# A list scheduler that counts DMA by packets and lanes, other places for the loads of z and v, and one pair of token blocks that stays in SBUF

## The chip, the cores and the metric

The kernel runs on one core of a Trainium2 chip. The metric is the device time of one execution in microseconds (us), the median of several runs. On the core work five engines with a queue of their own each: TensorE (PE in the profile) multiplies, VectorE (DVE) and ScalarE (ACT) do the elementwise work, GpSimd (POOL) and SyncE (SP) here mostly issue transfers.

## The reference

Three stages stand one behind the other. x is what one stage hands to the next: 6016 rows (tokens) of 256.

```
scores = (1/S) * z @ z.T                 # per batch, S = 3008, z is S x 64
x      = u * (maximum(scores, 0)**2 @ v) # attention, u and v are S x 256
g      = s * maximum(x @ w_in, 0)**2 + b # first MLP, 256 -> 2048
x      = g @ w_out                       # 2048 -> 256
h      = x @ w2_in                       # second MLP
out    = (h * sigmoid(1.702 * h)) @ w2_out
```

All of it is float32. No operand goes into TensorE as it is: each is split into a high part (a cast to a shorter format) and a low part (the rest), and a product is made of three matmuls: high by high, high by low, low by high. ACT makes the high parts (a cast, "hi"), DVE the low ones (a subtraction, "lo").

## The kernel before, in words

**Tiles.** The 3008 tokens of a batch are cut into five blocks of 512 and one of 448. The twelve blocks of both batches are numbered m = 0 to 11; 0 to 4 and the short 10 belong to the first batch, 5 to 9 and the short 11 to the second, and they are finished in the order 0, 1, 2, 3, 4, 10, 5, 6, 7, 8, 9, 11. For the MLPs two neighbours make a pair: pair p holds the blocks 2p and 2p+1, so pair 4 is blocks 8 and 9, and pair 5 the two short ones.

**Attention.** z is loaded transposed in pieces of 32 (tile zr, line 341), turned by DVE (zt, line 359), and split into zq and zk (lines 368 and 371 for zk). A tile holds the same 64 rows of z twice, in its upper and its lower 64 partitions. For the two first tiles of the first batch both halves are loaded; for the others the lower half is copied from the upper one by a transfer inside SBUF (line 351). Tiles of v are loaded (vr, line 411) and split (lines 427 and 431). Scores go into ps_s (line 511), are clipped and squared on ACT (lines 515 and 518), split (lines 522 and 526) and multiplied by v into accA or accB (lines 450, 451, 455). A score tile that another block needs transposed is turned by DVE (T, line 551), stored to DRAM (H<-T, line 566, POOL) and fetched again later (R<-H, line 579, SP) and split once more (lines 601 and 605). `gate` multiplies a block's sum by u (gx, line 911), `store_rows` writes it to DRAM, `fetch_rows` reads it again as f when its pair enters the first MLP.

**Weights.** While attention runs, the weights of both MLPs are prepared: `wr` is loaded (lines 632 to 638), taken apart and rounded on DVE and ACT (lines 645 to 732, "decode"), and stored in the forms that a seven-product scheme for 2 x 2 blocks needs (uf, dw, df, POOL). These operations are called free: nothing waits for them before the MLPs begin.

**MLPs.** For each layer and each pair, `up` (896 KB each, line 775) and `d` tiles are loaded, products go into ps_a to ps_d (line 1045), are combined, activated, split (lines 1164 and 1168) and multiplied down into the accumulators (line 1238). The last pair of the second layer ends the program: its parts are closed (line 1308), turned (line 984) and stored (line 997).

**What sets the order.** The program writes a list of operations with a cost each. `ordered` is a list scheduler: it runs through the list with a clock for each engine, its own prices for operations and transfers, due times that follow from what PE needs, and a count of free buffers (56 cells of 128 x 512, 13 "big", 5 "wide" ones, banks of the accumulators). It returns one fixed order for each engine. At run time only semaphores hold an instruction back, and an engine does not step past one that waits. SP issues loads, POOL issues stores. Each queue that issues DMAs goes round eight lanes: a DMA may wait for the one issued eight before it.

## Time and profile before

| | us |
|---|---|
| median of three runs (lowest, highest) | 1436.26 (1430.92, 1436.39) |
| the profiled execution | 1433.64 |
| its span, first to last instruction | 1431.9 |
| PE busy in the span | 1395.0 |
| DVE busy | 1312.7 |
| ACT busy | 1190.9 |

The profiled execution lies between the runs; 1.7 us of its time are outside the span. Busy PE is not PE at its peak, since a matmul at half clock counts as busy for longer. The rows of the trace use the line numbers of the kernel before.

### The profile page before, as it was taken

The page shows a single profiled execution, that of the slowest core. Times are in us where ns is not written, and L with a number is a line of the kernel's source. Part 1 is how long each engine was busy: PE and PEld are TensorE (multiplying, and loading weights), DVE is VectorE, ACT ScalarE, POOL GpSimd, SP SyncE. Part 2 cuts the span into 40 slices and gives each one's busy share as a digit, 9 for nine tenths or more (in the row PEclk, how much of TensorE's full clock was granted, in tenths as well). Part 3 has the DMA queues.
Part 4 walks back from the last instruction along what each step waited for, and adds up shares of the span by engine and source line. Part 5 has one row for each costly group of instructions (what it writes and reads, how often), then busy time and mean ns, then how long its engine had stood idle before and what let it go on. Part 6 is the DMA issues. An engine that isn't in the chain of part 4 may idle for free.

```text
span 1431.9 us, 20300 instructions
## 1 busy us (share of the span) xinstructions
PE 1395.0 (97%) x6147; PEld 1150.3 (80%) x6147; DVE 1312.7 (92%) x2324; ACT 1190.9 (83%) x2308; POOL 165.1 (12%) x260
## 2 busy tenths in 40 slices
PE   7999999999999799999999999999999999999997
PEld 4788889778887688887888778988887887878896
DVE  5998978999997699999999999898988999989996
ACT  6998866999876498998999898988888796968784
POOL 0022111131221100101001000000020202020201
PEclk9999999999999899999999999999999999999999
DMA  8698998688989976776757576666758474646644
GB/s 188 187 307 261 243 252 231 214 271 259 290 256 274 269 262 228 261 232 231 258 185 266 181 255 219 217 229 212 243 159 289 153 264 159 234 155 224 192 149 110
DMA packets 175949, 324.71 MB, mean 227 GB/s; under 512 B 61376, under 2 KB 96256, under 8 KB 172000
## 3 DMA queue, kind: packets, MB, share of 16 engines
q1 hardware_dynamic: 153104, 245.30, 56.6%
q0 software_dynamic: 19072, 77.45, 14.7%
q10 hardware_dynamic: 3664, 0.68, 0.3%
q8 instruction: 48, 0.79, 0.2%
q14 instruction: 61, 0.50, 0.1%
HBM read 243.93 MB, written 78.12 MB: 225 GB/s over the span
## 4 chain that ended last, share of the span: by engine, by line
PE 72%; DMA 8%; DVE 7%; issue 7%; ACT 4%; SPq 1%; POOL 1%; ACTq 0%; DVEq 0%; POOLq 0%
PE ps_d L1045 8%; PE ps_b L1045 7%; PE ps_c L1045 7%; PE accB L1238 6%; PE ps_b L1238 5%; PE ps_a L1045 4%; DMA R<-H 4%; PE accB L450 3%; PE accB L451 3%; PE ps_s L511 3%; PE accB L455 3%; PE accA L1238 3%; PE ps_c L1238 3%; PE accA L451 3%; PE accA L450 3%
## 5 line engine op out<-in xcount | busy, mean ns | idle before, releaser
L1168 DVE TENSOR_TENSOR lo<-g_c,hi 128x512 fp32r<-128x512 f32 (+1 forms) x540 | 346.1, 672 | 15.9 <-ACT hi L1164 15.2
L1164 ACT CAST hi<-g_c 128x512 fp32r<-128x512 f32 (+1 forms) x540 | 310.5, 618 | 3.7 <-DVE g_c L1153 1.2
L515 ACT ACTIVATE a<-ps_s 128x512 f32<-128x512 f32 (+1 forms) x168 | 100.2, 607 | 39.4 <-PE ps_s L511 39.3
L1045 PE MATMUL ps_b<-op_t,up 128*128 128x512 f32 (+1 forms) x432 | 121.3, 389 | 2.2 <-DVE g_c L1119 1.0
L1045 PE MATMUL ps_d<-op_t,up 128*128 128x512 f32 (+1 forms) x432 | 120.7, 387 | 0.4 <-DVE g_c L1119 0.4
L451 PE MATMUL accA<-hi,v 128*128 128x512 f32 x288 | 114.1, 396 | 6.2 <-DVE v L431 6.1
L450 PE MATMUL accB<-hi,v 128*128 128x512 f32 (+1 forms) x288 | 111.2, 386 | 5.2 <-ACT hi L522 5.2
L526 DVE TENSOR_TENSOR lo<-a,hi 128x512 fp32r<-128x512 f32 (+1 forms) x156 | 104.2, 672 | 11.5 <-ACT hi L522 11.0
L450 PE MATMUL accA<-hi,v 128*128 128x512 f32 x288 | 112.8, 392 | 0.5 <-ACT hi L522 0.2
L1131 ACT ACTIVATE g_c<-g_c 128x512 f32<-128x512 f32 (+1 forms) x144 | 89.5, 623 | 28.3 <-DVE g_c L1119 28.0
L451 PE MATMUL accB<-hi,v 128*128 128x512 f32 (+1 forms) x288 | 110.8, 385 | 0.0
L518 ACT ACTIVATE a<-a 128x512 f32<-128x512 f32 (+1 forms) x168 | 107.7, 650 | 1.1
L511 PE MATMUL ps_s<-zq,zk 128*128 128x512 f32 (+1 forms) x336 | 103.6, 395 | 4.5 <-DVE zk L371 3.9
L522 ACT CAST hi<-a 128x512 fp32r<-128x512 f32 (+1 forms) x168 | 105.7, 636 | 0.9
L1153 DVE TENSOR_TENSOR g_c<-g_c,g_c 128x512 f32<-128x512 f32 (+1 forms) x156 | 104.9, 672 | 1.5
L997 POOL DMA_DIRECT2D out_dram<-o x84 | 53.9, 649 | 404.1 <-DVE o L979 383.3
L1045 PEld LDWEIGHTS ps_b<-op_t,up 128*128 128x128 f32 x432 | 79.9, 188 | 21.5 <-DVE g_c L1119 3.4
L1238 PE MATMUL accB<-hi,d 128*128 128x512 f32 (+1 forms) x312 | 95.0, 386 | 0.0
L1045 PEld LDWEIGHTS ps_d<-op_t,up 128*128 128x128 f32 x432 | 80.4, 188 | 17.8 <-DVE g_c L1119 1.9
L1134 ACT ACTIVATE g_c<-g_c 128x512 f32<-128x512 f32 (+1 forms) x144 | 88.4, 629 | 0.7
L551 DVE STREAM_TRANSPOSE T<-a 128x512 f32<-128x512 f32 x120 | 83.9, 702 | 5.2 <-ACT a L518 4.8
L455 PE MATMUL accB<-lo,v 128*128 128x512 f32 (+1 forms) x276 | 83.8, 385 | 3.2 <-DVE lo L526 3.2
(172 smaller groups left out, 3460.0 us busy)
## 6 DMA issues: line engine op xcount, KB each, us to landing
up<-uf SPq DMA_DIRECT2D x96, 896.0 KB
H<-T POOLq DMA_DIRECT2D x30, 1024.0 KB, 7.2
R<-H SPq DMA_DIRECT2D x120, 256.0 KB
d<-dw SPq DMA_DIRECT2D x114, 256.0 KB
d_s<-df1s SPq DMA_DIRECT2D x54, 256.0 KB
f<-rows SPq DMA_DIRECT2D x20, 512.0 KB
d_s<-df0s SPq DMA_DIRECT2D x72, 128.0 KB
d_s<-df0s SPq DMA_DIRECT2D x36, 256.0 KB
```

What stands on the lines that cost most here:

```text
L450: nc.tensor.matmul(T[k][:, :n], w[:, 0, cols], T[hi][:, :n], **start_flags(k, fresh))
L451: nc.tensor.matmul(T[k][:, :n], w[:, 1, cols], T[hi][:, :n], **start_flags(k, ()))
L455: nc.tensor.matmul(T[k][:, :n], w[:, 0, cols], T[lo][:, :n], **start_flags(k, ()))
L511: nc.tensor.matmul(T[self.p][:, :n], k, T[zq][:, h, :n], start=h == 0, stop=h == 1)
L518: nc.scalar.activation(out=T[self.a][:, :n], in_=T[self.a][:, :n], func=AF.Square)
L522: nc.scalar.copy(out=T[self.hi][:, :n], in_=T[self.a][:, :n])
L526: nc.vector.tensor_tensor(out=T[self.lo][:, :n], in0=T[self.a][:, :n], in1=T[self.hi][:, :n], op=ALU.subtract)
L1045: nc.tensor.matmul(to[:, :n], a[h], y[:, g, :n], start=first and j == 0, stop=False, skip_group_check=True)
L1153: nc.vector.tensor_tensor(out=self.get(to), in0=self.get(x), in1=self.get(y), op=ALU.subtract)
L1164: nc.scalar.copy(out=T[keys[0]][:, :n], in_=self.get(c))
L1168: nc.vector.tensor_tensor(out=T[keys[1]][:, :n], in0=self.get(c), in1=T[keys[0]][:, :n], op=ALU.subtract)
L1238: nc.tensor.matmul(to[:, :n], w[:, h, cols], g[:, :n], start=first and j == 0, stop=False, skip_group_check=True)
```

## The change

The work on PE, DVE and ACT is the same, operation for operation (6147 matmuls before and now). What changes is the order, and some transfers.

1. **`ordered` and `moves`.** A transfer is now priced by its packets and its count of DMAs, with eight lanes per queue in the scheduler's model. A load is not placed earlier than `HOLD` = 4 us before the modelled transfer queue gets to it, unless it is due. The free decode operations get two windows each of the scheduler's clock in place of one: 45 to 235 and 300 to 370 us for the first layer's weights, 200 to 235 and 300 to 800 us for the second's (before: 20 to 450 and 200 to 800), and do not start ahead of the first.
2. **`load_z`.** In the first batch both halves of every tile are loaded from DRAM. In the second batch the copy inside SBUF is issued by POOL, not by SP.
3. **`load_v`.** The first batch's tiles of v but the first are issued by POOL.
4. **`KEPT` and `PAIRS`.** Blocks 8 and 9 are not stored and fetched again: the first MLP's operands are made from gate's own tile. Both MLPs take the pairs in the order 4, 0, 1, 2, 3, 5.
5. **`tail_of`.** For the pair that ends the program the products come in another order: one whole product (c11) behind P5 and P6 in place of ahead of P5, and c22 by halves at the end, beside c12.

```
+HOLD = 4
...
+            if op.pipe:
+                t = max(t, min(pipe - HOLD, latest[i] - 2.0), lanes[op.engine == "POOL"][0])
...
-        clocks[e] = s0 + op.cost
+        end, late = s0 + op.cost, op.late
+        if op.pipe:
+            time, land, lane = s0, 0.0, lanes[e == "POOL"]
+            for _ in range(op.count):
+                time = max(time, lane.pop(0))
+                pipe = max(pipe, time + 0.4) + op.pipe / op.count
+                time += op.cost / op.count
+                lane.append(max(time + 1.9, pipe + 1.7))
+                land = max(land, lane[-1])
+            end = time
+            late = land - end
...
-        twice = bb == 0 and t < 2
+        twice = bb == 0
...
-            move(128, lambda: nc.sync.dma_start(out=T[key][64:], in_=T[key][:64]), [key], [key])
+            move(128, lambda: nc.gpsimd.dma_start(out=T[key][64:], in_=T[key][:64]), [key], [key], engine="POOL")
...
+        queue = "POOL" if bb == 0 and c else "SP"
...
+    KEPT = (8, 9)
...
-        store_rows(0, m, key)
+        if m not in KEPT:
+            store_rows(0, m, key)
...
-        fs = [("f", layer, 2 * p + y) for y in range(2)]
+        fs = [("x" if layer == 0 and 2 * p + y in KEPT else "f", layer, 2 * p + y) for y in range(2)]
...
-        line = parts("c22", "P1") + late + whole("c11") + parts("t1", "P5")
+        line = parts("c22", "P1") + late
         if pair.ending:
-            line += parts("t2", "P6") + whole("c22") + parts("t3", "P7") + whole("c21")
+            line += parts("t1", "P5") + parts("t2", "P6") + whole("c11") + parts("t3", "P7") + whole("c21")
             line += close(0, 0, "v") + close(0, 1, "w")
             for d, x in enumerate(("s1", "u3")):
-                line += whole("c12", (d,)) + close(1, d, x)
+                line += whole("c22", (d,)) + whole("c12", (d,)) + close(1, d, x)
...
+    PAIRS = (4, 0, 1, 2, 3, 5)
...
-        [(20.0, 450.0), (200.0, 800.0)],
+        [[(45.0, 235.0), (300.0, 370.0)], [(200.0, 235.0), (300.0, 800.0)]],
```

Three places show what the new order is. A row is an instruction: its line, its kind, the tile it writes and what it reads. The first place is SP's queue at the very start; zr is z, vr is v, wr are the weights of the first MLP, and the number behind the name is the tile of the batch. Before:

```order
L341 DMA zr_2_185<-in_z_dram 32x16x32 x2
L411 DMA vr_1_188<-in_v_dram 32x4x256 x4
L341 DMA zr_3_193<-in_z_dram 32x16x32 x2
L411 DMA vr_2_199<-in_v_dram 32x4x256 x4
L636 DMA wr_0_214<-in_moe_w_in_dram 128x1x256 x2
L638 DMA wr_0_214<-in_moe_w_out_dram 128x512
L341 DMA zr_4_236<-in_z_dram 32x16x32 x2
L411 DMA vr_3_246<-in_v_dram 32x4x256 x4
L636 DMA wr_1_261<-in_moe_w_in_dram 128x1x256 x2
L638 DMA wr_1_261<-in_moe_w_out_dram 128x512
L351 DMA zr_2_185<-zr_2_185 64x512
```

and now:

```order
L356 DMA zr_0_168<-in_z_dram 32x16x32 x2
L356 DMA zr_1_178<-in_z_dram 32x16x32 x4
L429 DMA vr_0_183<-in_v_dram 32x4x256 x2
L356 DMA zr_2_203<-in_z_dram 32x16x32 x4
L356 DMA zr_3_232<-in_z_dram 32x16x32 x4
L356 DMA zr_4_289<-in_z_dram 32x16x32 x4
```

The copy of z tile 2 (L351) stood behind three loads of v and two of weights; now no copy is left in the first batch, the v tiles have gone to POOL, and the weights come behind all of z.

The second place is ACT's queue in the first microseconds, where v_0 and v_1 are the parts of the first and second tile of v. Before:

```order
L368 CAST zk_0_206<-zt_0_197 128x512
L427 CAST v_0_0_210<-vr_0_175 128x256
L427 CAST v_0_1_212<-vr_0_175 128x256
L427 CAST v_0_2_219<-vr_0_175 128x256
L427 CAST v_0_3_225<-vr_0_175 128x256
L515 ACTIVATE a<-ps_s 128x512 x2
```

and now:

```order
L445 CAST v_1_0_201<-vr_1_171 128x256
L445 CAST v_1_1_208<-vr_1_171 128x256
L383 CAST zk_0_212<-zt_0_193 128x512
L445 CAST v_1_2_215<-vr_1_171 128x256
L445 CAST v_1_3_218<-vr_1_171 128x256
L383 CAST zk_1_230<-zt_1_221 128x512
L533 ACTIVATE a<-ps_s 128x512 x2
```

Two casts of the second tile of v, which POOL loads now, stand ahead of the cast of zk_0 that the first scores need. On DVE one subtraction of the same tile (v_1_0) stands likewise ahead of the two that the first scores need.

The third place is SP's queue where attention ends; R_5 are the last stored score tiles that block 11 fetches, f_0 and f_1 the stored rows of the pair that was first, ur is u. Before:

```order
L579 DMA R_5_1_4905<-H_5_1_3920 32x4x512 x4
L579 DMA R_5_2_5029<-H_5_2_4295 32x4x512 x4
L856 DMA f_0_5097<-rows_0_123 128x1024
L856 DMA f_1_5120<-rows_1_124 128x1024
L579 DMA R_5_3_5188<-H_5_3_4675 32x4x512 x4
L775 DMA up_0_0_5214<-uf_75 128x1792
L632 DMA wr_7_5226<-in_moe_w_in_dram 128x2x256
L638 DMA wr_7_5226<-in_moe_w_out_dram 128x512
L579 DMA R_5_4_5236<-H_5_4_5034 32x4x512 x4
```

and now:

```order
L650 DMA wr_7_5130<-in_moe_w_in_dram 128x2x256
L656 DMA wr_7_5130<-in_moe_w_out_dram 128x512
L597 DMA R_5_2_5150<-H_5_2_4287 32x4x512 x4
L597 DMA R_5_3_5205<-H_5_3_4695 32x4x512 x4
L597 DMA R_5_4_5253<-H_5_4_5010 32x4x512 x4
L793 DMA up_4_0_5304<-uf_75 128x1792
L793 DMA up_4_1_5332<-uf_76 128x1792
```

The two f loads are gone, the last weight tile has moved ahead of R_5_2, and the first `up` load behind R_5_4.

## Rows read from the trace of the kernel before

**Rows 1.** Page of the kernel: busy time of each engine.

```profile
PE 1395.0 (97%) x6147; PEld 1150.3 (80%) x6147; DVE 1312.7 (92%) x2324; ACT 1190.9 (83%) x2308; POOL 165.1 (12%) x260
```

**Rows 2.** Windows: stretch, length, busy us of five engines, granted clock, DMA share, GB/s.

```profile
36.00:99.40 63.40, 62.32 (x268) 49.23 (x268) 63.03 (x121) 61.99 (x124) 9.92 (x16) 1.00 0.80 243
99.40:240.00 140.60, 140.60 (x633) 118.45 (x632) 120.64 (x226) 107.24 (x206) 19.39 (x30) 1.00 0.91 247
274.00:292.00 18.00, 16.80 (x66) 11.57 (x65) 17.88 (x40) 17.61 (x39) 4.97 (x8) 1.00 0.66 226
446.00:482.00 36.00, 27.12 (x111) 22.10 (x111) 25.02 (x46) 20.12 (x41) 2.70 (x4) 0.86 1.02 259
482.00:1421.80 939.80, 934.14 (x4159) 776.46 (x4158) 879.39 (x1496) 800.23 (x1538) 84.41 (x130) 1.00 0.64 217
```

**Rows 3.** Timeline of the first 13 us: start, duration, engine, instruction, [idle before it].

```profile
0.75 0.91 SPq L341 DMA_DIRECT2D zr<-in_z_dram  x2
...
4.53 0.71 DVE L359 STREAM_TRANSPOSE zt<-zr 128x512 f32<-128x512 f32 x1 [3.34 <-DMA zr<-in_z_dram]
...
6.72 1.33 ACT L427 CAST v<-vr 128x256 fp32r<-128x256 f32 x4 [0.83 <-DMA vr<-in_v_dram]
...
7.27 2.20 PE L511 MATMUL ps_s<-zq,zk 128*128 128x512 f32 x8
...
12.05 1.20 PE L511 MATMUL ps_s<-zq,zk 128*128 128x512 f32 x4 [2.57 <-DVE zk L371]
```

**Rows 4.** Timeline from 20 to 34 us, the copy of z and what waits.

```profile
27.89 0.71 DVE L359 STREAM_TRANSPOSE zt<-zr 128x512 f32<-128x512 f32 x1 [5.00 <-DMA zr<-zr]
...
28.64 0.62 ACT L368 CAST zk<-zt 128x512 fp32r<-128x512 f32 x1 [4.94 <-DVE zt L359]
...
28.96 0.79 PE L451 MATMUL accA<-hi,v 128*128 128x512 f32 x1 [5.06 <-DVE v L431]
...
33.96 0.62 ACT L368 CAST zk<-zt 128x512 fp32r<-128x512 f32 x1 [3.18 <-DVE zt L359]
```

**Rows 5.** Timeline of the end of attention, 455 to 482 us.

```profile
455.78 4.70 SPq L579 DMA_DIRECT2D R<-H  x4
461.46 1.67 ACT L601 CAST hi<-R 128x512 fp32r<-128x512 f32 x3 [3.55 <-DMA R<-H]
470.15 0.43 DVE L645 TENSOR_SCALAR pw<-wr 128x512 uint32<-128x512 uint32 x1 [3.08 <-DMA wr<-in_moe_w_out_dram]
471.50 1.11 PE L455 MATMUL accB<-lo,v 128*128 128x448 f32 x2 [3.20 <-DVE lo L526]
474.76 0.62 ACT L601 CAST hi<-R 128x512 fp32r<-128x512 f32 x1 [7.14 <-DMA R<-H]
476.79 0.74 PE L450 MATMUL accB<-hi,v 128*128 128x448 f32 x1 [4.18 <-ACT hi L522]
```

**Rows 6.** Timeline of DVE, two neighbours in a stretch without idle time.

```profile
442.26 0.68 DVE L526 TENSOR_TENSOR lo<-a,hi 128x512 fp32r<-128x512 f32 x1
442.86 0.41 DVE L682 TENSOR_TENSOR zeros<-zeros,wf 128x256 f32<-128x256 f32 x1
```

**Rows 7.** POOL's group of stores (busy us, mean ns), and DMA issue to landing.

```profile
L997 POOL DMA_DIRECT2D out_dram<-o x84 | 53.9, 649 | 404.1 <-DVE o L979 383.3 <-DVE o L984 16.4 <-DVE g_c L1153 3.7
...
out_dram<-o POOLq DMA_DIRECT2D x80, 64.0 KB, 4.8
```

**Rows 8.** Timeline of the last 12 us.

```profile
1419.51 0.99 PE L1213 MATMUL accA<-hi,d 128*128 128x448 f32 x4
...
1420.27 0.62 DVE L1296 TENSOR_TENSOR k_w<-ps_d,k_p 128x448 f32<-128x448 f32 x1 [4.38 <-ACT k_u L1280]
...
1421.78 0.37 PE L1213 MATMUL accB<-lo,d 128*128 128x448 f32 x1
...
1424.55 0.60 DVE L984 STREAM_TRANSPOSE o<-k_u 128x448 f32<-128x448 f32 x1
```

**Rows 9.** Waits of SP's queue from 482 to 1421.8 us: total, times, longest.

```profile
SPq L775 <- PE ps_d L1045: 267.2, 44, 15.3
```

More of the change, by code (lines that the diff above doesn't have):

```diff
@@ L92, in ordered @@
     extra = [i for i in range(n) if ops[i].free]
-    for which, (a, b) in enumerate(spread):
+    for which, windows in enumerate(spread):
         some = [i for i in extra if ops[i].free == which + 1]
+        whole = sum(b - a for a, b in windows)
         for x, i in enumerate(some):
-            latest[i] = a + (b - a) * x / len(some)
+            t = whole * x / len(some)
+            for a, b in windows:
+                if t < b - a:
+                    break
+                t -= b - a
+            latest[i] = a + t
     for i, op in enumerate(ops):
@@ L110, in ordered @@
     waiting = [len(b) for b in before]
-    ready, calm = [0.0] * n, [0.0] * n
+    ready, calm = [0.0] * n, [spread[op.free - 1][0][0] if op.free else 0.0 for op in ops]
     pending = {e: [] for e in clocks}
@@ L185, in ordered @@
                 u[1] -= 1
-                u[2] = max(u[2], s0 + op.cost + late)
+                u[2] = max(u[2], end + late)
                 if u[1] == 0:
@@ L192, in ordered @@
             waiting[j] -= 1
-            t = s0 + (lag(i, j) if not op.pipe else op.cost + late)
+            t = end + late if op.pipe else s0 + lag(i, j)
             ready[j] = max(ready[j], t)
@@ L280, in attention_mlp_mlp_kernel, with put @@
     ops, T = [], {}
-    def put(engine, cost, late, f, reads=(), writes=(), new=(), adds=(), free=0, due=None, pipe=0, soon=None):
-        ops.append(Op(engine, cost, late, f, reads, writes, new, adds, free, due, pipe, soon))
+    def put(engine, cost, late, f, reads=(), writes=(), new=(), adds=(), free=0, due=None, pipe=0, soon=None, count=1):
+        ops.append(Op(engine, cost, late + pipe, f, reads, writes, new, adds, free, due, pipe, soon, count))
     def scalar(n, f, reads=(), writes=(), new=(), **more):
@@ L289, in vector, with moves @@
         put("DVE", 0.065 + (0.00056 if fast else 0.00105) * n, 0.14, f, reads, writes, new, **more)
-    def carry(kb, run):
-        return kb * 1024 / run * (0.0185 + run / 27200) / 16
     STORES = "POOL"
     to_hbm = dict(SP=nc.sync, POOL=nc.gpsimd)[STORES]
-    def move(kb, f, reads=(), writes=(), new=(), engine="SP", run=2048, **more):
-        put(engine, 0.75 if engine == "POOL" else 0.45, 2.0, f, reads, writes, new, pipe=carry(kb, run), **more)
-    def moves(kb, fs, reads=(), writes=(), new=(), engine="SP", run=2048, count=None, **more):
+    def moves(kb, fs, reads=(), writes=(), new=(), engine="SP", run=2048, count=None, slow=1.0, **more):
         def f():
@@ L303, in f, with move @@
                 g()
-        put(engine, (0.75 if engine == "POOL" else 0.45) * (count or len(fs)), 2.0, f, reads, writes, new, pipe=carry(kb, run), **more)
+        count = count or len(fs)
+        pipe = 1.05 * slow * kb * 1024 / run * (0.0085 + run / 27200) / 16
+        put(engine, (0.7 if engine == "POOL" else 0.45) * count, 2.0, f, reads, writes, new, pipe=pipe, count=count, **more)
+    def move(kb, f, *args, **more):
+        moves(kb, [f], *args, **more)
     def matmuls(count, n, f, reads=(), adds=(), writes=(), new=()):
@@ L1513, in write_list @@
         for layer in range(2):
-            for p in range(NP):
+            for p in PAIRS:
                 parity[layer, p] = flip
```

43 lines of the change are left out of this document (22 added, 21 removed).

## The prediction, made before the change was run

> **What bounds the kernel now.** I read the page first. PE is busy for 1395.0 of 1431.9 us [rows 1], so some 37 us of the span are without a matmul, and the matmuls that ran at half clock come on top. No work leaves PE, so the question is which of these microseconds the new order gives back. Windows show that they are not spread evenly. From 99 to 240 us PE is never idle [rows 2]. In the 940 us of the MLPs it misses 5.7 (939.80 less 934.14), 0.6%. What is left lies in four places: the first 60 us, a small one near 280, the end of attention, and the last 10 us.
>
> *The start.* A timeline shows DVE waiting 5.00 us, until 27.89, for the copy of a z tile inside SBUF, and ACT 4.94 us for the turned tile; PE then starts again after 5.06 us [rows 4]. Another copy costs ACT 3.18 us more, until 33.96 [rows 4]. From 36 to 99 us DVE has 0.4 us of idle time and ACT 1.4, PE 1.1 [rows 2]: these two set the pace until they have caught up. So what the copies cost is what the two engines that pace the stretch lost, 4.94 + 3.18 = 8.1 us, and not the larger gap on PE.
>
> *Near 280.* Between 274 and 292 us DVE works 17.88 of 18.00 us, ACT 17.61, and PE misses 1.2 [rows 2].
>
> *The end of attention.* Of 36 us from 446 on PE misses 8.9, at a mean granted clock of 0.86 [rows 2]. The 0.86 are 36 x 0.14 = 5.0 us of lost clock; the level is half (1.2 GHz) for twice that, some 10 us, from about the matmul at 471.50 that followed 3.20 us of waiting. As 4.2 to 4.8 of these 10 us were idle in any case, the slow matmuls themselves cost some 2.6. Loss here: 8.9 + 2.6 = 11.5. The chain is read backwards: PE waits 4.18 us for a cast on ACT; ACT stood before it for 7.14 us until 474.76 at a cast of R, for the transfer issued from 455.78 on; and PE's 3.20 us came from DVE, which stood for 3.08 us at a weight tile [rows 5]. An engine in program order that waits for a late load holds up the small split behind it, for which PE waits.
>
> *The last 10 us.* The last matmul starts at 1421.78, the last turn of DVE ends at 1425.15 [rows 8], and transfers run to 1431.9.
>
> **The change part by part.**
>
> *z and v, first 60 us.* Every z tile of the first batch comes from DRAM in whole, and no load waits for another: the 8.1 us of waits go. Against it, the first scores now stand behind the second tile of v, from POOL. POOL issues four DMAs at 0.65 us each [rows 7] from about 0.8 us, so until 3.4. For the landing I have no row of this load. The quick end is the first z tile: issued until 1.7, turned at 4.53 [rows 3], 2.9 us. The slow end is POOL's small stores in full traffic, 4.8 us [rows 7]. So it lands at 6.3 to 8.2. Then one cast of 256 columns on ACT (four take 1.33, so 0.33 [rows 3]), and on DVE one subtraction of 256 and two of 512, at most 0.41 and, by the starts in [rows 6], 0.60 each: together 1.9 us, first scores at 8.2 to 10.1 in place of 7.27 [rows 3]. Part of the 0.9 to 2.8 comes back: the four casts of v no longer stand between the cast of zk_0 and that of zk_1, and the 2.57 us at 12.05 [rows 3] shrink as the second tile of z is loaded at once. I take 1.2 us net (bounds 0 and 2.2). The matmuls that idle to keep PE warm end at about 7.6, so PE waits 0.6 to 2.5 us; after the 2.57 us at 12.05 the next ones ran at full clock (four in 1.20) [rows 3], after 5.06 at half (one in 0.79) [rows 4], so I expect full clock. Sum of the start: 8.1 - 1.2 = 6.9 us gained.
>
> *A rule that speaks against loads on POOL.* POOL issues 84 stores at 649 ns each [rows 7], most of them in the MLPs, where DVE is busy for 879 of 940 us [rows 2]: no trace of a hold-up. The Trainium skill's SBUF page (SBUF — State Buffer, "SBUF: two separate sides") says that some VectorE instructions lock GpSimd out, so that it cannot write the descriptors of its transfers. By that rule each of the 19 issues could be late by one DVE instruction; the ones that count run while DVE does two of them, so the sum would be worse by at most about 1 us. The row decides: nothing.
>
> *Decode windows.* The order of the change puts more decode between the gates of the first and the fifth block (before at 99 and 240 us): 65 in place of 44 DVE instructions of 512, 14 for 8 of 256, 41 for 27 of 128. At 0.60 for the first and at most 0.41 for the others [rows 6] that is 12.6 + 8.2 = 20.8 us at most, on 120.64 of 140.60 us [rows 2]: DVE becomes full, by this upper bound 0.8 us over. That costs little if each split is ready in time, and everything that DVE then waits for lands on PE. I put 2 us (bounds 0 and 7, all that the start gained). In exchange nothing is decoded from 235 to 300 in the scheduler's clock, and the 1.2 us near 280 go.
>
> *End of attention.* Before, 0.9 MB of `up` and 0.5 MB of weights were issued between the last two fetches of R, and two f loads (1 MB) ahead of them. ACT stood for the one fetch until 461.46 and for the next until 474.76 [rows 5]; in these 13.3 us came 0.9 + 0.5 + 1.0 = 2.4 MB. Behind one another the last megabyte takes 1.0 / 2.4 x 13.3 = 5.5 us, so it is there at 467.0 if the fetch before it is not earlier, and at 464 or sooner if the missing f loads help. ACT asked for it at 467.62 (474.76 - 7.14) [rows 5]. The 7.14 us go, if narrowly. The weight tile lies ahead of R_5_2 now, so DVE's 3.08 us go too. The wait of 3.55 us for the fetch before it stays in part; PE lost about 1.3 us by that. Block 9's operands move into this stretch on DVE, which has 11 us of idle time there [rows 2]; I leave another 1.2. So 11.5 - 2.5 = 9.0 us gained (bounds 4 and 11.5). What is late next is `up` for the first product, issued behind R; its first matmul was at 489.5, 22 us after the time that I give R_5_4, and 0.9 MB take 5.
>
> *Tail.* The last join on DVE starts at 1420.27, and from there nine operations follow without a gap until 1425.15 [rows 8]. In the new order 18 matmuls follow the product that it joins, in place of 12. Those 12 start from 1419.51 to 1421.78, 0.206 apart [rows 8], so the join comes 1.2 us sooner against the end of PE. I take 1.2 (0 to 2).
>
> *Copies of the second batch.* They go to POOL, behind stores that wait for DVE; a late one would hold DVE and ACT as the 5.00 us did [rows 4]. The cover is that they stand in the order ahead of the gate of block 4, while the second batch's scores come behind it: nothing (bound 5).
>
> *The MLPs* keep their operations; loads change places. PE's waits there are 5.7 us in all [rows 2], so little can be gained; I put nothing.
>
> **Sum**, against the profiled execution's 1433.64: -6.9 + 2 - 1.2 - 9.0 - 1.2 = -16.3, so 1417.3. That execution is 2.6 below the median of the three runs, inside their spread, and I let its level stand: 1417.
>
> **The rivals.** (a) *The stall at the end of attention only changes its cause*: the fetch is issued late since its buffer is not free, or DVE, which now makes pair 4's operands there, holds up the splits. For it: the transfers are busy all through the stretch (share 1.02 [rows 2]). 1417 + 9 = 1426. (b) *DVE binds the first half*: it has no slack left in 140 us by my count, and what it waits is lost. The 7 us of the start are eaten: 1424. Against it: the 20.8 are an upper bound, since the smallest instructions of the decode are counted at the price of twice their width. (c) *All gains at their upper end*: 8.1 + 1.2 + 11.5 + 2 = 22.8, 1411, and some of the MLPs' 5.7 on top: 1406 to 1411. (d) *Slower*: SP's queue is in order, and each `up` load waits in it until PE has let go of a buffer (44 of these waits for ps_d alone take 267 us, 6 each [rows 9]). Loads that are held back and then stand behind such a wait come late. With 96 `up` loads the gain is gone when each is late by 16.3 / 96 = 0.17 us on PE, and at 0.25 the time is 1441. Against it: no wait of PE for a load is seen in the MLPs, and the loads are issued a whole buffer ahead. (e) *Neither place pays*, (a) and (b) together: 1433.
>
> **How the numbers follow.** Forecast (1411 to 1423) 0.54; (a) 0.15; (b) 0.12; (c) 0.10; (d) 0.05; (e) 0.04. The range reaches to (c) on one side and a little past (a) on the other: 1405 to 1430 leaves out (d), (e) and the edges of the others, under 2 in 10. Runs of one kernel here lie up to 5.5 us apart, so about 0.5% (7 us) tells from no change: faster means below 1429. The forecast, (c), (b) and most of (a) lie there, 0.87; within 7 us (e) and the rest, 0.08; slower (d), 0.05.
>
> **What would show it.** No idle time of DVE for a copy of z in the first 40 us, first scores between 8.2 and 10.1, and the gate of the first block some 6 to 7 us sooner than 99; PE without a gap from 93 to 233, with DVE full; no cast of R that waits for 7 us, PE at full clock through the end of attention, with under 4 us of waits; last turn of DVE about 2 us after the last matmul. I am wrong if PE shows waits for splits between 100 and 240, if ACT or DVE stands at a load of R or at an operand before 480, or if PE waits for `up` or `d` in the MLPs.

## The result and the profile after

| | us |
|---|---|
| change, median of four runs (lowest, highest) | 1413.78 (1413.02, 1415.66) |
| before, four runs of the same comparison | 1434.55 (1430.92, 1436.39) |
| ratio, with its 95% interval | 0.986 (0.9836 to 0.9885) |
| profiled execution of the change, its span | 1413.4, 1411.5 |

The change is faster by 1.4%, 3.2 us under the forecast of 1417. The two profiled spans differ by 20.4 us (1431.9 and 1411.5). The page's row of busy times, to be read against [rows 1]:

```profile
PE 1390.5 (99%) x6147; PEld 1151.0 (82%) x6147; DVE 1313.9 (93%) x2324; ACT 1191.6 (84%) x2308; POOL 179.5 (13%) x283
```

PE's busy time fell by 4.5 us with the same 6147 matmuls, so fewer of them ran at half clock. Time without a matmul fell from 36.9 to 21.0 us. Windows of the change (columns as in [rows 2]):

```profile
36.00:99.40 63.40, 62.91 (x272) 50.13 (x271) 61.97 (x120) 63.00 (x127) 9.42 (x15) 1.00 0.80 255
99.40:240.00 140.60, 137.74 (x612) 115.66 (x612) 125.06 (x246) 105.24 (x205) 26.33 (x41) 0.99 0.92 258
211.00:218.00 7.00, 7.00 (x24) 5.61 (x25) 5.71 (x10) 1.66 (x3) 1.99 (x3) 0.76 1.05 313
240.00:300.00 60.00, 57.73 (x249) 45.74 (x248) 57.89 (x114) 52.99 (x114) 10.08 (x17) 1.00 0.85 256
446.00:482.00 36.00, 36.00 (x175) 32.45 (x174) 29.17 (x58) 22.55 (x45) 9.19 (x13) 1.00 0.97 327
482.00:1403.50 921.50, 918.62 (x4092) 763.81 (x4090) 871.41 (x1475) 796.58 (x1526) 79.37 (x122) 1.00 0.63 215
```

From 99 to 240 us, where PE never stood before [rows 2], it now misses 2.86 us, and 2.27 more up to 300. From 446 on, where it missed 8.88 at a clock of 0.86, it misses nothing. In the MLPs it misses 2.9 us (921.50 less 918.62), before 5.7.

**Where the 20.4 us lie.** A window of fixed times holds other work in another order, so I also counted by work. For every matmul in the trace I took the time from its start to the next start, less what it takes where nothing disturbs (0.2267 us with 512 columns, 0.200 with 448). The rest is lost time, from idle PE or half clock. The stages are cut where PE has done 85, 300 and 500 us of undisturbed work: A is the start, B the rest of the first batch's attention and the start of the second's, C the end of attention and the first MLP's beginning, D the MLPs to the last matmul, and E what follows it. In us:

| kernel | A | B | C | D | E | span | median | ratio to before (95%) |
|---|---|---|---|---|---|---|---|---|
| before | 18.8 | 4.4 | 14.9 | 17.6 | 10.1 | 1431.9 | 1434.55 | |
| the change | 12.9 | 10.2 | 0.9 | 13.5 | 8.0 | 1411.5 | 1413.78 | 0.986 (0.9836 to 0.9885) |
| difference | -5.9 | +5.8 | -14.0 | -4.1 | -2.1 | -20.4 | | |

One experiment below (the old tail) has the change's order up to the tail; its stages A to D come out within 0.5 us of the change's, which says how far such a number can be trusted. Each row of the stages is read from one execution, while whole runs of one kernel lie up to 5.5 us apart. Up to 300 us of work both kernels lost the same, 23.2 and 23.1 us: what the start gave, stage B took back. The whole gain was made behind it.

The next fence is the timeline of the change (start, duration, engine, instruction, idle time before it) in four stretches: the first 17 us, 190 to 213, 233 to 254, and the last 12. The text below goes through them in this order.

```profile
1.38 5.04 POOL L429 DMA_DIRECT2D vr<-in_v_dram  x9 [0.51 <-issue]
...
9.16 0.71 ACT L445 CAST v<-vr 128x256 fp32r<-128x256 f32 x2 [4.87 <-DMA vr<-in_v_dram]
...
11.40 5.06 PE L529 MATMUL ps_s<-zq,zk 128*128 128x512 f32 x11 [3.64 <-DVE zk L386]
...
190.33 0.53 SPq L654 DMA_DIRECT2D wr<-in_moe_w_in_dram  x1
191.40 4.39 SPq L656 DMA_DIRECT2D wr<-in_moe_w_out_dram  x1
...
208.21 0.43 DVE L663 TENSOR_SCALAR pw<-wr 128x512 uint32<-128x512 uint32 x1 [5.90 <-DMA wr<-in_moe_w_out_dram]
...
210.83 0.74 PE L473 MATMUL accA<-lo,v 128*128 128x512 f32 x2 [2.86 <-DVE lo L544]
...
212.22 0.63 PE L469 MATMUL accA<-hi,v 128*128 128x512 f32 x1
...
233.86 1.13 POOL L366 DMA_DIRECT2D zr<-zr  x2 [20.87 <-PE accB L473]
...
238.41 1.02 ACT L445 CAST v<-vr 128x256 fp32r<-128x256 f32 x3 [4.58 <-DMA vr<-in_v_dram]
238.86 0.71 DVE L374 STREAM_TRANSPOSE zt<-zr 128x512 f32<-128x512 f32 x1 [3.66 <-PE accB L473]
...
253.23 0.50 PE L468 MATMUL accA<-hi,v 128*128 128x512 f32 x1 [1.20 <-DVE gx L930]
...
1400.05 0.97 PE L1233 MATMUL accA<-hi,d 128*128 128x448 f32 x4
...
1400.82 0.62 DVE L1316 TENSOR_TENSOR k_w<-ps_d,k_p 128x448 f32<-128x448 f32 x1 [3.81 <-ACT k_u L1300]
...
1403.49 0.37 PE L1233 MATMUL accB<-lo,d 128*128 128x448 f32 x1
...
1405.09 0.60 DVE L1004 STREAM_TRANSPOSE o<-k_u 128x448 f32<-128x448 f32 x1
```

**The start.** ACT stands 4.87 us for the second tile of v, which POOL loads; the cast of zk_0 is queued behind it, and the first scores start at 11.40, not 7.27 [rows 3]. Eleven matmuls then take 5.06 us, 0.46 each: half clock. The view of DMA issues gives POOL's loads of v in the first 20 us (count, KB each, median us from issue to landing), and between 225 and 260 its copies of z:

```profile
vr<-in_v_dram POOLq DMA_DIRECT2D x16, 128.0 KB, 6.4
...
zr<-zr POOLq DMA_DIRECT2D x6, 128.0 KB, 4.8
```

No wait for a copy of z follows in the first 60 us, and PE and both elementwise engines stay nearly full from 36 on.

**Stage B** has two places. SP issued the last two loads of a weight tile at 190.33 and 191.40, DVE asked for it at 202.31 (208.21 less 5.90) and stood until 208.21. The small subtraction behind it was late, PE stood 2.86 us, and from 212.22 on matmuls ran at half clock. The second place is the start of the second batch: POOL issued the copies of two tiles at 233.86, and DVE turned the first at 238.86 after 3.66 us of idle time. The row names a matmul as the releaser, but the copy's issue and the 4.8 us of its kind to landing end at 238.7, so I read it as the copy, and e6 below bears that out. ACT stood 4.58 us for a tile of v, and the next gate held PE for 1.20. PE's three longest waits of the first 330 us, by the view of waits (total, times, longest), say the same:

```profile
PE ps_s L529 <- DVE zk L386: 3.6, 1, 3.6
PE accA L473 <- DVE lo L544: 2.9, 1, 2.9
PE accA L468 <- DVE gx L930: 1.7, 2, 1.2
```

**The tail**, the last rows of the timeline: the join on DVE starts at 1400.82, 2.67 us ahead of the last matmul (before 1.51 [rows 8]), and the last turn 1.60 behind it (before 2.77).

### The profile page after: what moved, and what is told of

Its sections match the earlier page's. It is cut to its first block, busy times and chain, and to the rows that moved or that the text cites. A ratio compares the mean times of both kernels' runs of the same rounds, so it can differ in the third digit from the quotient of the medians.

```text
span 1411.5 us, 20355 instructions
## 1 busy us (share of the span) xinstructions
PE 1390.5 (99%) x6147; PEld 1151.0 (82%) x6147; DVE 1313.9 (93%) x2324; ACT 1191.6 (84%) x2308; POOL 179.5 (13%) x283
## 4 chain that ended last, share of the span: by engine, by line
PE 83%; DMA 6%; issue 5%; ACT 4%; DVE 1%; POOL 1%; SPq 0%; POOLq 0%; DVEq 0%; ACTq 0%
PE ps_d L1065 8%; PE ps_c L1065 8%; PE ps_b L1065 8%; PE accB L1258 7%; PE ps_b L1258 6%; PE ps_d L1258 4%; PE accB L469 4%; PE accB L468 4%; PE accB L473 4%; PE ps_a L1065 4%; PE ps_s L529 4%; PE ps_c L1258 3%; PE accA L1258 3%; PE accA L469 3%; PE accA L468 3%
## 5 line engine op out<-in xcount | busy, mean ns | idle before, releaser
L533 ACT ACTIVATE a<-ps_s 128x512 f32<-128x512 f32 (+1 forms) x168 | 104.1, 622 | 25.4 <-PE ps_s L529 25.2
L536 ACT ACTIVATE a<-a 128x512 f32<-128x512 f32 (+1 forms) x168 | 111.4, 666 | 0.9
L540 ACT CAST hi<-a 128x512 fp32r<-128x512 f32 (+1 forms) x168 | 109.1, 651 | 0.7
L473 PE MATMUL accA<-lo,v 128*128 128x512 f32 x276 | 85.7, 392 | 2.9 <-DVE lo L544 2.9
```

The costliest lines, as they stand in the source:

```text
L473: nc.tensor.matmul(T[k][:, :n], w[:, 0, cols], T[lo][:, :n], **start_flags(k, ()))
L536: nc.scalar.activation(out=T[self.a][:, :n], in_=T[self.a][:, :n], func=AF.Square)
L540: nc.scalar.copy(out=T[self.hi][:, :n], in_=T[self.a][:, :n])
```

## The experiments

Each changes the kernel of the change, except two that change the kernel before. The texts on record name the theories that each run was to tell apart. Stages are those of the table above; ratios are to the kernel before, run anew beside each set of experiments (medians from 1433.95 to 1436.26). So medians of two experiments that lie some 2 us apart can't be told from one another.

| run | A | B | C | D | E | span | median | ratio (95%) |
|---|---|---|---|---|---|---|---|---|
| e1 old tail | 13.0 | 10.2 | 0.9 | 14.0 | 10.0 | 1414.1 | 1416.20 | 0.9878 (0.9862 to 0.9893) |
| e2 old pair and pair order | 12.8 | 9.7 | 2.2 | 19.7 | 8.0 | 1418.4 | 1422.80 | 0.9926 (0.9910 to 0.9943) |
| e3 old windows | 14.3 | 9.1 | 2.3 | 14.1 | 8.1 | 1413.9 | 1416.30 | 0.9875 (0.9855 to 0.9896) |
| e4 v by SP | 9.9 | 12.5 | 0.9 | 14.0 | 7.7 | 1411.0 | 1412.58 | 0.9851 (0.9836 to 0.9865) |
| e5 old DMA reckoning | 13.6 | 9.6 | 1.1 | 20.4 | 8.1 | 1418.8 | 1420.96 | 0.9891 (0.9875 to 0.9908) |
| e6 z copied, by SP | 12.9 | 6.2 | 0.9 | 16.8 | 7.6 | 1410.5 | 1413.13 | 0.9844 (0.9829 to 0.9858) |
| e7 no decode before 300 | 12.0 | 0.5 | 62.4 | 19.3 | 8.3 | 1468.5 | 1470.39 (one) | |
| e8 v by SP, slack 12 | 8.0 | 14.8 | 0.8 | 24.3 | 7.7 | 1421.6 | 1422.42 | 0.9907 (0.9892 to 0.9922) |
| e9 before + kept pair | 19.7 | 5.3 | 7.9 | 13.6 | 10.2 | 1422.7 | 1423.46 | 0.9921 (0.9906 to 0.9935) |
| e10 before + windows | 10.3 | 10.7 | 1.3 | 18.4 | 10.2 | 1416.9 | 1419.68 | 0.9898 (0.9882 to 0.9914) |
| e11 v and copies by SP | 9.2 | 10.0 | 0.8 | 14.6 | 7.8 | 1408.4 | 1409.11 | 0.9825 (0.9811 to 0.9840) |
| e12 the same, slack 8 | 9.2 | 15.9 | 4.6 | 22.8 | 7.8 | 1426.3 | 1427.56 | 0.9946 (0.9930 to 0.9963) |

### The tail alone: e1

```
-        line = parts("c22", "P1") + late
+        line = parts("c22", "P1") + late + whole("c11") + parts("t1", "P5")
         if pair.ending:
-            line += parts("t1", "P5") + parts("t2", "P6") + whole("c11") + parts("t3", "P7") + whole("c21")
+            line += parts("t2", "P6") + whole("c22") + parts("t3", "P7") + whole("c21")
...
```

> The changed kernel with the old order of products in the last pair; the order of every other instruction ahead of it is the same. Main theory (the join on VectorE comes 6 matmuls sooner, and the transfers behind it too): 1.2 to 2 us slower than the changed kernel, 1415 to 1416, with the span from the last matmul to the end about 10 us in place of 8. Rival (the end is set by the last transfers, whatever the order): 1413.5 to 1414, the span behind the last matmul still 8 us or the loss before it smaller by as much.

Stage E goes from 8.0 back to 10.0 and nothing else moves by more than 0.5. The tail is worth 2.0 us in the profile, against 1.2 forecast.

### The start: e6, e4

e6 copies z inside SBUF again, in the first batch too, and lets SP issue all copies.

```
-        twice = bb == 0
+        twice = bb == 0 and t < 2
...
-            move(128, lambda: nc.gpsimd.dma_start(out=T[key][64:], in_=T[key][:64]), [key], [key], engine="POOL")
+            move(128, lambda: nc.sync.dma_start(out=T[key][64:], in_=T[key][:64]), [key], [key])
```

> The changed kernel with the old loading of z: from the third tile on, the lower half of a tile is copied from the upper one inside SBUF by SyncE, but the copies now stand right behind the loads of z. Theory A (a copy costs a second landing, wherever it stands): VectorE waits 3 to 6 us for the third tile of z, 3 to 5 us slower by 90 us than the changed kernel. Theory B (the copies were late only since loads of v and of weights stood ahead of them): no wait for a copy over 1 us, TensorE's lost time at 90 us within 1 us of the changed kernel's, 1412 to 1415.

The copies are back and stage A stays at 12.9. DVE's longest waits of the first 60 us in e6, by the view of waits, hold no copy:

```profile
DVE v L449 <- ACT v L445: 3.8, 1, 3.8
DVE zt L374 <- DMA zr<-in_z_dram: 3.5, 1, 3.5
DVE lo L544 <- ACT hi L540: 2.1, 3, 1.1
```

So loading z twice bought nothing here. In e6 no load of weights or of v stands ahead of a copy in SP's queue any more. e10 (below) narrows it down: the kernel before, with its copies, loses 10.3 us in stage A when decode starts at 45, and DVE has no wait for a copy there either. Its timeline of SP's queue still has loads of v ahead of the first copy, at 16.58, but the first weight tile behind all of z:

```profile
12.71 3.83 SPq L417 DMA_DIRECT2D vr<-in_v_dram  x8
16.58 0.57 SPq L357 DMA_DIRECT2D zr<-zr  x1
...
24.31 1.29 SPq L642 DMA_DIRECT2D wr<-in_moe_w_in_dram  x2
```

So of the loads ahead it is the weights whose move counts; that e10 also keeps the decode's own work off DVE and ACT until 45 may be part of its 10.3, and no run separates the two. The copy had been late twice over: in the kernel before it was issued at 20.39 (next row), 3.8 us later than in e10, and used 7.5 us after that, at 27.89 [rows 4]; in e10 DVE turned this tile at 21.32 without a wait, 4.7 us after the issue.

```profile
20.39 0.55 SPq L351 DMA_DIRECT2D zr<-zr  x1
```

e6 also takes 4.0 us out of stage B, the part at the start of the second batch (there the tile of z is turned after a wait of 0.48 us in place of 3.66, although SP issued its copy no sooner than POOL did, as a timeline of e6 shows):

```profile
234.11 1.17 SPq L366 DMA_DIRECT2D zr<-zr  x2
...
236.46 0.71 DVE L374 STREAM_TRANSPOSE zt<-zr 128x512 f32<-128x512 f32 x1 [0.48 <-DMA zr<-zr]
```

D grew by 3.3, so the medians hardly differ, 1413.13 and 1413.78.

e4 lets SP load all of v.

```
-        queue = "POOL" if bb == 0 and c else "SP"
+        queue = "SP"
```

> The changed kernel with all tiles of v issued by SyncE, in between those of z; the casts of the second tile of v no longer stand ahead of the first scores. Main theory (the 4 us by which the first scores come later are lost at the start and can be had back): first scores at 7 to 8 in place of 11.4, full clock there, 2 to 4 us gained by 90 us; how much of it lasts depends on the waits at 207 and 250: 1410 to 1413. Rival (ScalarE and VectorE set the pace until 90 us, and work that is done sooner waits for the later tiles of z and v): first scores sooner, but the gate of the first block at 98 as now, 1413 to 1416.

The first scores start at 7.60 and eight of them take 2.11 us, full clock, as a timeline of e4 shows:

```profile
7.60 2.11 PE L529 MATMUL ps_s<-zq,zk 128*128 128x512 f32 x8 [0.41 <-DVE zk L386]
```

Stage A falls by 3.0, B rises by 2.3. The start gained what the late first scores had cost; the stretch behind it, where the decode lies, took most of it back.

### What takes the start's gain: e7, e8

e7 keeps all decode out of the first 300 us.

```
-        [[(45.0, 235.0), (300.0, 370.0)], [(200.0, 235.0), (300.0, 800.0)]],
+        [[(300.0, 450.0)], [(300.0, 800.0)]],
```

> The changed kernel with no weights decoded before 300 us of the list's clock, so that neither VectorE nor the transfers carry that work in the first batch. Only TensorE's lost time up to 300 us is read; later the decode is late and the whole is slower, 1420 to 1450. Theory A (what is lost between 85 and 300 us, about 10 us in the changed kernel, comes from decode work and its transfers, the wait of 5.9 us for a weight tile above all): at most 3 us lost there. Theory B (the second batch's first block is paced by ScalarE and VectorE, or by its loads of z and v, whatever else runs): 4 us or more still lost between 230 and 300.

Stage B loses 0.5 us instead of 10.2. So without decode and its transfers stage B's loss does not arise, the second batch's start included; e6 takes 4.0 of it away with the decode in place, so for that part the queue of the copies matters too. The price is 62.4 us in stage C, where the decode is then crowded, and 1470 us in all, more than the 1420 to 1450 of the text. A window of e7 shows what the stretch is like without decode: PE never idle, DVE busy 96.45 of 142 us, the transfers at a share of 0.68. The second row is from e7's view of DMA issues between 205 and 240: POOL's copies of the second batch's z land after 2.2 us there, where the change's took 4.8.

```profile
98.00:240.00 142.00, 142.00 (x642) 120.16 (x641) 96.45 (x156) 96.85 (x186) 8.52 (x16) 1.00 0.68 174
...
zr<-zr POOLq DMA_DIRECT2D x6, 128.0 KB, 2.2
```

e8 is e4 with a larger margin: the scheduler places a decode operation no sooner than 12 us behind the modelled landing of its load (before 5).

```
-SLACK = (5.0, 1.0, 0.5)
+SLACK = (12.0, 1.0, 0.5)
```

> All tiles of v by SyncE as before, and in the list 12 us in place of 5 between the modelled landing of a transfer and the free decode operation that waits for it. Theory A (the stalls that are left in attention are in-order engines that stand at a decode operation whose load landed later than modelled; 12.4 us from issue to landing where TensorE lost 4.8 us): the wait at 207 goes, 3 to 5 us gained against all v by SyncE, 1406 to 1410. Rival (a decode operation that is placed later moves its stall to another place): 1411 to 1415.

The wait for a weight tile is gone from the list of DVE's waits between 95 and 300, and stage B still rose, to 14.8. Its longest wait there is now 7.29 us, at the start of the second batch, by a timeline of e8:

```profile
230.87 1.15 POOL L366 DMA_DIRECT2D zr<-zr  x2 [18.00 <-DMA zr<-in_z_dram]
...
234.40 0.71 DVE L374 STREAM_TRANSPOSE zt<-zr 128x512 f32<-128x512 f32 x1 [7.29 <-DMA ur<-in_u_dram]
...
244.84 0.69 DVE L386 TENSOR_TENSOR zk<-zt,zk 64x512 fp32r<-64x512 f32 x1
...
245.67 0.77 PE L529 MATMUL ps_s<-zq,zk 128*128 128x512 f32 x1 [5.67 <-DVE zk L386]
```

The row names a load of u, but what is turned is z, whose copy POOL issued at 230.87. Behind it DVE worked through fifteen decode operations before the subtraction of zk at 244.84, for which PE stood 5.67 us. D rose to 24.3. So margin alone is no cure. My theory that it would be fell; the rival, that the stall moves to another place, held in kind, but the cost was far above its 1411 to 1415.

### The end of attention: e9, e10, e2, e3, e5

e9 is the kernel before with only the kept pair and the order of pairs, its core:

```
+    KEPT = (8, 9)
...
+        if m not in KEPT:
+            store_rows(0, m, key)
...
+    PAIRS = (4, 0, 1, 2, 3, 5)
```

> The kernel before with one part of the change alone: blocks 8 and 9 stay in SBUF and the pairs go 4, 0, 1, 2, 3, 5. SyncE's queue at the end of attention is that of before without the two loads of rows; up and the last weight tile still stand between the last two fetches. Theory A (the two loads of rows, 1 MB, are what made the last fetch late): the last fetch is there 5 us sooner, TensorE loses 6 or less there in place of 14.6, 1424 to 1429. Theory B (the loads of up and of weights between the fetches, and the wait for the weight tile on VectorE, made it): 10 us or more still lost there, 1430 to 1436.

Stage C falls from 14.9 to 7.9, between the two theories and nearer to A. The f loads are gone, but `up` and the last weight tile still stand between the fetches. ACT still stands at two fetches of R, 2.14 and 5.12 us where it was 3.55 and 7.14 [rows 5], by a timeline of e9:

```profile
457.55 1.66 ACT L601 CAST hi<-R 128x512 fp32r<-128x512 f32 x3 [2.14 <-DMA R<-H]
...
468.31 0.62 ACT L601 CAST hi<-R 128x512 fp32r<-128x512 f32 x1 [5.12 <-DMA R<-H]
```

e10 is the kernel before with only the decode windows (and the rule that decode doesn't start ahead of its first one).

```
-    ready, calm = [0.0] * n, [0.0] * n
+    ready, calm = [0.0] * n, [spread[op.free - 1][0][0] if op.free else 0.0 for op in ops]
...
-        [(20.0, 450.0), (200.0, 800.0)],
+        [[(45.0, 235.0), (300.0, 370.0)], [(200.0, 235.0), (300.0, 800.0)]],
```

> The kernel before with one part of the change alone: the new windows for the decode, with the old reckoning of transfers, the old loads and the old pairs. The last weight tile stands ahead of the last three fetches now, up between the last two. Theory A (decode that leaves the second half takes its loads out of the way of the fetches): under 4 us lost at the end of attention in place of 14.6, but 4 to 10 more lost between 85 and 280 us; 1426 to 1434. Theory B (the windows only matter together with the other parts): 10 us or more lost at the end of attention, 1434 to 1442.

Stage C falls to 1.3, with the f loads still ahead of the last fetches (issued at 392.7 and 398.5, before at 441.81) and `up` between the last two. That is theory A, and B rose by 6.3 as it says; its 1426 to 1434 were missed at 1419.68, since stage A fell by 8.5 as well. A window of e10 shows PE full and the transfers at 0.81 in place of 1.02 [rows 2]:

```profile
446.00:482.00 36.00, 36.00 (x175) 32.68 (x174) 27.19 (x55) 19.76 (x38) 4.18 (x6) 1.00 0.81 239
```

Three runs undo one part each in the change: the kept pair (e2: `KEPT = ()`, `PAIRS = (0, 1, 2, 3, 4, 5)`), the windows (e3: `[[(20.0, 450.0)], [(200.0, 800.0)]]`), and the reckoning of DMAs (e5), whose core is

```
-                t = max(t, min(pipe - HOLD, latest[i] - 2.0), lanes[op.engine == "POOL"][0])
...
+            pipe = max(pipe, end) + op.pipe
+            late = max(late, pipe + 3.0 - end)
```

> The changed kernel, but no pair stays in SBUF, and the pairs go 0 to 5; the two loads of rows for the first pair stand ahead of the last weight loads and of the last three fetches, which stay next to each other. Theory A (the two loads of rows, 1 MB, fed the stall at the end of attention): the waits for the last fetches come back, 5 to 9 us of idle TensorE between 440 and 480, 1419 to 1423. Theory B (what fed it was that the loads of up and of weights stood between the last fetches): idle time of TensorE there stays under 2 us, 1413 to 1416.

> The changed kernel with the old windows for the decode of the weights: 62 in place of 86 VectorE instructions of 512 before the gate of the fifth block. Theory A (the 10 us that TensorE loses between 85 and 280 us come from the decode that was moved there): these fall to about 4 as before, and the second half loses at most 2 more, 1407 to 1411. Theory B (the lighter second half is what took the stall at the end of attention away): the first half gains 6, but 8 to 14 us of idle TensorE come back between 400 and 480, 1414 to 1422.

> The changed kernel with the old reckoning of transfers in the list: the old prices, no lanes, no packets, no holding back. The loads of z and v, the kept pair, the windows and the tail stay as changed. Theory A (the order that the new reckoning gives SyncE's queue took away the stall at the end of attention): 6 to 14 us of TensorE lost there again, 1420 to 1430. Theory B (the lighter second half, or the loads that are gone, did): under 2 us lost there, 1412 to 1417.

None brings stage C back: 2.2, 2.3 and 1.1. The stall at the end of attention has several remedies in this change, and any two of the three nearly suffice. When SP issued the last fetch of R goes with it in part: by 444 us in the change, e2, e5 and e10, at 456.6 in e9 and 460.5 in the kernel before; but e3, at 457.2, lost only 2.3. e3 met neither of its theories in size: the old windows cost 2.5 us in all (medians 1416.3 and 1413.8), spread over A and C, with B only 1.1 better, so the windows are not all of what stage B loses. Where e2 and e5 lose is stage D, 6.2 and 6.9 us above the change, which neither text had put there as the larger part. (e6, which touches neither the pairs nor the reckoning, loses 3.3 more there too.) In e2 one of the waits is long enough to be seen in the view of waits of PE behind 540 us:

```profile
PE ps_d L1065 <- ACT s_u L1114: 2.7, 1, 2.7
```

It comes at 679 us, where ACT and DVE stand for a store of decoded forms. In e5 the single waits are under 1 us.

### A version that beats both: e11, e12

e11 is the change with v (as e4) and the second batch's copies (as e6) issued by SP; the first batch's z is still loaded twice.

> The changed kernel with both new uses of POOL's queue undone: all tiles of v, and the copies of the second batch's z, are issued by SyncE; z of the first batch still comes from DRAM in whole. Theory A (POOL's queue makes both late: 3 us at the start, 4 us where the second batch begins): both gains add up, 1405 to 1409. Rival (where the second batch begins, VectorE and ScalarE are behind in any case, and what is gained before is lost there): lost time at 300 us is again 22 to 23, 1411 to 1414.

Its four runs' median is 1409.11, with the highest at 1411.19, below the lowest of the change (1413.02); 4.7 us under the change and 1.75% under the kernel before. The gain is stage A's 3.7 for the most part: B is 2.5 below e4 but hardly below the change, so the two gains did not add up in full. First scores start at 6.89. Windows of e11 by the same amounts of work as the stages A to C:

```profile
0.00:94.40 94.40, 90.60 (x376) 68.45 (x377) 86.44 (x164) 88.60 (x181) 10.93 (x23) 1.00 0.79 232
94.40:319.40 225.00, 219.96 (x968) 181.85 (x968) 207.66 (x401) 181.94 (x362) 37.94 (x59) 0.99 0.89 258
319.40:520.10 200.70, 200.70 (x905) 169.12 (x903) 185.68 (x353) 161.33 (x311) 34.81 (x53) 1.00 0.90 263
```

All that is left of stalls up to 520 us is in the first two: 3.8 and 5.0 us idle. DVE's two longest waits of the second are a weight tile again and a copy of z:

```profile
DVE pw L663 <- DMA wr<-in_moe_w_out_dram: 12.4, 4, 5.6
DVE zt L374 <- DMA zr<-zr: 2.8, 1, 2.8
```

e12 tries a margin between the two, `SLACK = (8.0, 1.0, 0.5)`, on e11.

> As the one before, with 8 us in place of 5 between the modelled landing of a transfer and the decode operation that waits for it. Theory A (the wait of VectorE for a weight tile near 207 us goes, and with the copies on SyncE it is not lost again where the second batch begins): 3 to 5 us better than with 5, 1402 to 1406. Rival (the decode that is placed later stalls the engines in the MLPs): the wait near 207 goes, but 3 us or more come back behind 480, 1406 to 1412.

It is 18.5 us slower than e11: stage B 15.9, C 4.6, D 22.8. ACT's longest wait between 190 and 300 us shows one part of it, a tile of v for the second batch:

```profile
ACT v L445 <- DMA vr<-in_v_dram: 9.0, 2, 7.5
```

Both of its theories' times are missed by far (1402 to 1406, 1406 to 1412). With e8 this is the second time that a larger margin for the decode loads moved the loss and raised it.

## Why the prediction was right, and where its steps were not

The forecast and its range held: 1413.8 in 1405 to 1430. The sum was nearly right, -16.3 against -20.4 of span, but two of its terms erred by 5 us in opposite directions, and one place was left out. That the sum came so near is luck in part. Of the signs of being wrong that I had named, one came: PE waited for a split between 100 and 240 us, the 2.86 us until 210.83.

1. **Start, -6.9; measured -5.9 in stage A.** The size was right, the step "the 8.1 us of waits go" because no copy is left was not. e6 has the copies and the same stage A; e10 has them in the old kernel, with loads of v ahead of them, and loses only 10.3. What made a copy late was the weights ahead of it in SP's queue; moving those loads is what counts. The rows of SP's queue shown with the change have the weights behind z, but I credited the doubled loads. The mark that I had named, the gate of the first block 6 to 7 us sooner, was a poor one: it came at 98.17, 1.3 us sooner, with more matmul work ahead of it. By work, 85 us of it were done at 98.1 in place of 104.1.
2. **First scores at 8.2 to 10.1, at full clock; measured 11.40, half clock.** The step that failed is the landing of the second tile of v, put at 6.3 to 8.2: ACT cast it at 9.16. The slow end, the 4.8 us of POOL's stores [rows 7], was too short for this load: POOL's loads of v took 6.4 from issue to landing. With 3.64 us of idle time in place of at most 2.5, the expectation of full clock fell too. e4 prices both: 3.0 us in A, where I had put 1.2 with a bound of 2.2.
3. **Decode windows, +2 and -1.2 near 280; measured +5.8 in stage B.** This is the term that was mis-sized, and its mechanism was another. I asked whether DVE has enough time, counted 20.8 us at most and found it full. It was not full: 125.06 busy in the window where I expected some 141. Block 4's gate came at 252.52, not 239.96, so the work was spread over a longer stretch. DVE stood for a *load* instead. Between 95 and 300 us the view of its waits begins with weight tiles and the late z:

```profile
DVE pw L663 <- DMA wr<-in_moe_w_out_dram: 10.4, 4, 5.9
DVE zt L374 <- PE accB L473: 3.7, 1, 3.7
```

   The longest wait is the 5.90 us at 208, of which PE paid 2.86 idle and, in half clock, some 1.7 (3.4 us at that level, last section, are worth half of it). e7 shows that stage B's loss does not arise without the decode, and e6 that 4.0 of it sit at the start of the second batch (point 4). That the new windows make it is only half shown: they alone raise B by 6.3 in the kernel before (e10), but the change with the old windows still loses 9.1 there (e3). The place near 280 did clear: between 245 and 300 us of work the kernel before lost 4.0 and the change 1.1; between 85 and 245 they lost 0.4 and 9.1. The bound of 7 did hold the sum. Rival (b), DVE as the bound, has the right place and price (the 7 us of the start eaten) but the wrong cause.
4. **Copies of the second batch, nothing (bound 5); measured 2.5 to 4 of stage B.** "They stand in the order ahead of the gate of block 4" was true and did not help: POOL issued them at 233.86, and DVE stood 3.66 us for the tile. They were not held up behind stores, as I had feared: POOL had issued nothing since 213. With the copies on SP (e6), issued at 234.11, that wait is 0.48. With v on SP as well the step is smaller, 2.5 us of stage B (e4 and e11).
5. **End of attention, -9.0 (bounds 4 and 11.5); measured -14.0 in stage C.** The stretch from 446 to 482, which I had priced at 11.5, lost 13.2 by the count by work and now loses 0.4. The reason given, the f loads and `up` out of the way, is half the story: the f loads alone give 7.0 (e9), and e10 loses 1.3 with `f` and `up` both still ahead of the last fetch. The windows alone give 13.6 (e10), a cause that I had booked only as a cost. Which megabyte counted cannot be told apart in the change itself, since undoing any one part leaves 2.3 us or less.
6. **Tail, -1.2 (0 to 2); measured -2.1,** and 2.0 by e1. The join came 1.16 us sooner against the end of PE, as worked out. The rest lies behind the last turn: from its start to the end of the span 6.4 us in place of 7.3.
7. **MLPs, 0; measured -4.1.** I had looked at PE's listed waits only (5.7 us) and taken them for all that could be had. The order of pairs and the kept pair alone give 4.0 (e9) and undoing them costs 6.2 (e2); undoing the reckoning costs 6.9 (e5). That rival (d), loads held back too long, did not come about is seen in the waits: behind 466 us none of PE's is for a load. Of the 4.1, 2.8 are idle time of PE (5.7 less 2.9). Stage D also rose by 3.3 in e6, which changed only transfers of z, so other orders of the same pairs cost as much, and no run shows what in the order counts. Which stalls the reckoning avoids I can't name; they are many and short, and this stays open.
8. **POOL held up by DVE, nothing; measured nothing in the issues, open for the landings.** The group of POOL's stores in the change (its row stands below) takes 652 ns each, with DVE busy for 95% of the MLPs (871.41 of 921.50), where it was 649 [rows 7]. The rule of the Trainium skill (SBUF — State Buffer, "SBUF: two separate sides") that some VectorE instructions lock GpSimd out has again no trace in the issues: the nine at the start took 5.04 us, 0.56 each. But what was late in points 2 and 4 was the landing and not the issue, and the row of issues can't decide that. POOL's copies landed after 4.8 us with the decode and after 2.2 without it (e7), which would fit such a hold-up as well as traffic, and SP's copy that took 7.5 us in the kernel before shows that a copy can be as late without POOL; no run separates the two.

```profile
L1017 POOL DMA_DIRECT2D out_dram<-o x84 | 54.1, 652 | 396.6 <-DVE o L999 387.8 <-DVE o L1004 6.8 <-DVE k_u L1328 1.1
```

Undone one at a time, the parts are worth, in medians: the pair and its order 9.0 us, the reckoning 7.2, the windows 2.5, the tail 2.4; the doubled z with POOL's copies and v on POOL come out at a cost of 0.6 and 1.2, too little to tell from nothing; by the ratios to the kernel before, which ran beside each, the reckoning comes out at about 4.5 (0.9891 against 0.986), by the spans at 7.3. v and the second batch's copies together back on SP bring 4.7. The parts don't add up, because several of them remove the same stall: windows alone bring 14.9 to the kernel before, the pair alone 11.1.

## What to carry to other kernels

Work that "nothing waits for" still stands in an engine's queue: when its load is late, the urgent instruction behind it is late too, so ask of free work when its data land and what is queued behind it, not only how long it takes. When a transfer is late, look at what stands ahead of it in the same queue before you blame the transfer; here moving the weight loads did what doubling the z loads was credited with. Compare two orders by the work done, not by the clock: at 300 us of matmul work the two kernels had lost the same 23 us, which no window of fixed times shows.

## What the runs showed of the hardware

- A short idle time can be followed by half clock. Before, 2.57 us of idle time left the clock full [rows 3]. In the change PE stood 2.86 us until 210.83, ran for 1.1 us at full clock and then at half; the window from 211 to 218 above shows the mean of the two levels, 0.76, and 7.0 x 0.24 x 2 = 3.4 us at half clock. The Trainium skill (TensorE: Matmul & The Clock Gate, "Part 1: The HAM clock gate") says that this clock gate has two states, 1.2 and 2.4 GHz; the starts of the matmuls in this stretch, 0.23 or 0.43 us apart, agree. In e11 an idle time of 2.08 us, shorter than the one that left the clock full, was also followed by half clock (granted 0.50 from 675 to 678, timeline and window below), so here the length of the idle time alone does not tell which it will be.

```profile
673.56 0.98 PE L1065 MATMUL ps_c<-op_t,up 128*128 128x512 f32 x3 [2.08 <-DVE g_c L1139]
...
675.00:678.00 3.00, 3.00 (x8) 1.96 (x7) 2.90 (x5) 3.00 (x7) 0.00 (x0) 0.50 0.02 9
```

- A load can take long under traffic: the weight tile at 208 was issued by 195.8 at the latest (191.40 and 4.39 us) and used as soon as it was there, 12 us later, with the transfers at a share of 0.92 between 99 and 240. A copy of z, 128 KB inside SBUF, took 4.8 us to land when POOL issued it at the start of the second batch, while one that SP issued there from 234.11 on (e6) was used at 236.46. It isn't the queue alone: with no decode about (e7) POOL's copies landed after 2.2 us, and SP's copy of 20.39 in the kernel before was used 7.5 us after its issue.
